# Low-rank mix in a fused attention and mixer kernel: second products placed two channel tiles at a time, sums of u issued later

## The chip, the cores and the metric

The kernel runs on one core of one Trainium2 chip. Its time is the device time of one execution in microseconds (us): 680.91 us, the median of three runs (680.91 to 682.74). The core has a matrix engine (PE, with its weight loads, PEld), a vector engine (DVE), a scalar engine (ACT), a general engine (POOL) and a queue that starts DMAs (SP). Each works through its own instructions in the order in which the program issues them, and they wait for each other through semaphores.

## The reference

Clustered attention over 2 batches of 768 tokens and 8 heads gives a tensor x of 2 x 768 x 512. Two mixers follow. The first ends with a channel mix, and the second has a low-rank token mix of rank 32 and a feed-forward with 2048 inner channels:

```
u = x + y                                  # first mixer, y from the token mix
x = u + relu(u @ w_ch)                     # channel mix
h = x^T @ U @ V                            # low-rank token mix: 768 -> 32 -> 768
u = x + h^T
out = u + relu(u @ w_ch1) @ w_ch2          # feed-forward
```

Everything is float32. A float32 product is made of three matmuls on reduced-precision halves (high with high, high with low, low with high).

## The kernel before, in words

x is kept as eight tiles xT[b * 4 + t], 128 channels by 768 tokens, four channel tiles t for each batch b. The change lies in the function mixer, in the stretch between the channel mix and the first products of the feed-forward. An order written out by hand decides there; no planner moves instructions. These helpers matter:

- chmix(b, e, mid), L582 and L587: 24 matmuls into two PSUM banks, one per half of the tokens, and then two DVE instructions that add the positive part to xT. In the middle of its matmuls it calls mid.
- turn(b, t), L600 and L601: six PE transposes of one channel tile into two banks, copied out by two ACT instructions.
- low1(b), L627 to L635: the first product of the low-rank mix, 48 small matmuls into one bank. ACT copies it out (L631, four instructions), DVE and ACT split it into halves (L633, L634, L635).
- low2(b, t), L644 and L646: the second product for one channel tile, two matmuls into a bank each, each added to xT by one DVE instruction.
- split_u(b, t), L651 and L652: ACT makes the high half of u (768 columns), POOL the low half.
- u_sum(0, i), L664: two DVE subtractions each, of tiles that both lie in SBUF. The sums 1 to 4 feed a seven-product scheme for 2 x 2 blocks (class Quartet, L744 and L752) whose first use is Quartet(1, 0). Sum 2 reads sum 1, and sum 4 reads sum 2.
- split_sum(0, i), L670 and L671: ACT makes the high half of a sum, POOL the low half.
- ff1(c, f, mid), L698 to L705: 12 matmuls into one bank (512 columns), then gh by ACT (L703) and gl by DVE (L705). The bank is free when gl is made.
- ff2(c, f), L717: three matmuls for each of four channel tiles e, into four banks that ff2(0, 0) takes and ff2(0, 1) gives back after its additions (L727).
- conv_step and conv_after: a background conversion of the next weights. conv_after holds finished steps that are still to be issued. Just ahead of chmix(1, 0) it holds three: three POOL additions (L467 to L469), and two splits, each an ACT instruction (L473) and a POOL instruction (L475).
- unit(n), L796: second products of a Quartet. unit(0) of Quartet(1, 0) reads g[0, 0] and g[1, 0], which POOL makes at L758.

PSUM has eight banks that are handed out in a ring: a new tile takes the bank that was handed out eight tiles earlier and waits until that one has been read. Only ff2 keeps its four banks out of the ring.

```
    ring = deque(range(8))
    def bank(name, keep=None):
        i = ring.popleft()
        if keep is None:
            ring.append(i)
```

Of the kernel before, what the change touches and what calls it, by code (L numbers as in the profile page):

```python
# [23 lines left out]
NP = 4  # L24
# [17 lines left out]
def tile_cluster_block(ctx: ExitStack, tc: tile.TileContext, qk, v, cent, wth, wr, wi, wch,  # L42
# [69 lines left out]
    def cols(hf):  # L112
        return slice(hf * HALF, (hf + 1) * HALF)
# [324 lines left out]
    def conv_until(dst, i):  # L438
        while i not in dst:
            assert conv_do or conv_in or conv_load or conv_after  # L440
            conv_step()
# [131 lines left out]
    def chmix(b, e, mid=None):  # L573
        ps = banks("h")
        n = 0
        for t in range(NP):
            if mid and t == 2:
                mid()
            wv = wcol(wch_t, t * DM + e * P, P)
            for a, c in PASSES:  # L580
                for hf in range(2):
                    nc.tensor.matmul(out=ps[hf][:, :HALF], lhsT=wv[a], rhs=xs[b, t][c][:, hf * HALF:(hf + 1) * HALF],  # L582
                                     start=(n == 0), stop=(n == 11))
                n += 1
        x = xT[b * NP + e]
        for hf in range(2):
            nc.vector.scalar_tensor_tensor(x[:, cols(hf)], ps[hf][:, :HALF], 0.0, x[:, cols(hf)], op0=ALU.max, op1=ALU.add)  # L587
# [4 lines left out]
    def turn(b, t):  # L592

        x = xT[b * NP + t]
        xt4[b, t] = slot(f"xt{t}", F32, [P, NT, P])
        for hf in range(2):
            ps = bank("tp")
            for j in range(3):
                st = 3 * hf + j
                nc.tensor.transpose(ps[:, j * P:(j + 1) * P], x[:, st * P:(st + 1) * P], ident)  # L600
            nc.scalar.activation(out=xt4[b, t][:, 3 * hf:3 * hf + 3].rearrange("p s d -> p (s d)"), in_=ps[:, :HALF],  # L601
                                 func=AF.Copy)
# [20 lines left out]
    def low1(b):  # L623
        ps = bank("h1")
        for st in range(NT):
            for t in range(NP):
                nc.tensor.matmul(out=ps[32 * t:32 * t + 32, :P], lhsT=uv["u"][:, st * RANK:(st + 1) * RANK],  # L627
                                 rhs=xt4[b, t][:, st], start=(st == 0), stop=(st == NT - 1))
        h1 = slot("h1")
        for t in range(NP):  # L630
            nc.scalar.activation(out=h1[0:32, t * P:(t + 1) * P], in_=ps[32 * t:32 * t + 32, :P], func=AF.Copy)  # L631
        hs = slot("h1s", F32R)
        nc.vector.tensor_copy(hs[0:32, :DM], h1[0:32, :DM])  # L633
        nc.vector.tensor_tensor(hs[64:96, :DM], h1[0:32, :DM], f32(hs[0:32, :DM]), op=ALU.subtract)  # L634
        nc.scalar.activation(out=hs[32:64, :DM], in_=h1[0:32, :DM], func=AF.Copy)  # L635
        h1s[b] = hs
# [50 lines left out]
    def ff1(c, f, mid=None):  # L687
        ps = bank("g")
        o = 0
        for b, s0, w in CHUNKS[c]:  # L690
            n = 0
            for t in range(NP):
                if mid and t == 2:
                    mid()
                conv_until(w1p_t, f)
                wv = [w[:, t * P:(t + 1) * P] for w in w1p_t[f]]
                for a, e in PASSES:
                    nc.tensor.matmul(out=ps[:, o:o + w], lhsT=wv[a], rhs=us[b, t][e][:, s0:s0 + w],  # L698
                                     start=(n == 0), stop=(n == 11))
                    n += 1  # L700
            o += w
        gh = tmp.tile([P, 512], F32R, tag="gh", name="gh")
        nc.scalar.activation(out=gh, in_=ps, func=AF.Relu)  # L703
        gl = tmp.tile([P, 512], F32R, tag="gl", name="gl")
        nc.vector.scalar_tensor_tensor(gl, ps, 0.0, f32(gh), op0=ALU.max, op1=ALU.subtract)  # L705
        gt[c, f] = (gh, gl)
# [309 lines left out]
    def mixer():  # L1016

        seq = [(u, st) for u in range(4) for st in range(NT)]
        LEAD = 2
        CONVERT = (*range(3, 16), 20, 21)  # L1020
        last = NG - 1
        for n in range(len(seq) + LEAD):
            if n < len(seq):
                theta(*seq[n])
                if 3 <= n < 22:
                    conv_step()
                theta_z(*seq[n])
            if n >= LEAD:
                ymix(*seq[n - LEAD])
            if n == 1:  # L1030
                row_sums(last)
            if n == 2:
                spread(last)
                norm_x(last)
            if n in CONVERT:
                conv_step()
            if n < len(seq):
                theta_lo(*seq[n])
            if n in CONVERT:
                conv_step()  # L1040
            if n in (9, 10):
                for t in range(2):
                    split_x(1, 2 * (n - 9) + t)
            if n == 11:
                conv_load.extend(weigh_in(wch, NP * DM, wch_t))
                c2 = weigh_in(w2, NF * DM, w2_t)
                ff = []
                for k in range(NQ):
                    if k < GF // 2:
                        ff.extend(Convert(w1, NF * DM, 2 * k + j, keep_split(w1p_t), width=DM) for j in range(2))  # L1050
                    else:
                        ff.extend(weigh_pair(k))
                    while c2 and c2[0].c0 < (k + 1) * 2 * DM:
                        ff.append(c2.pop(0))
                conv_load.extend(ff[:4])
                conv_load.append(Convert(u_in, NT * RANK, 0, [keep_u]))
                conv_load.append(Convert(v_in, S, 0, [keep_v, keep_vl], 32))
                conv_load.extend(ff[4:])
                conv_start()
            if 20 <= n <= 23:  # L1060
                split_x(0, n - 20)
            if n in (24, 25):
                split_x(1, n - 24, nc.gpsimd)

        for e in range(NP):
            chmix(0, e, lambda: e and turn(0, e - 1))
            if e in (0, 1):
                split_x(1, 2 + e)
            conv_step(3)
        conv_until(uv, "u")  # L1070
        conv_until(uv, "v")
        while conv_after:
            conv_after.popleft()()
        chmix(1, 0, lambda: turn(0, 3))
        low1(0)
        chmix(1, 1, lambda: turn(1, 0))
        conv_step(3)
        for t in range(NP):
            low2(0, t)
        for t in range(NP):  # L1080
            split_u(0, t)
        chmix(1, 2, lambda: turn(1, 1))
        u_sum(0, 1)
        u_sum(0, 2)
        chmix(1, 3, lambda: turn(1, 2))
        split_sum(0, 1, nc.gpsimd)
        split_sum(0, 2, nc.gpsimd)
        u_sum(0, 3)
        u_sum(0, 4)
        ff1(0, 0, lambda: turn(1, 3))  # L1090
        low1(1)
        split_sum(0, 3, nc.gpsimd)
        split_sum(0, 4, nc.gpsimd)
        ff1(0, 1)
        for t in range(NP):
            low2(1, t)
        ff2(0, 0)
        for t in range(NP):
            split_u(1, t)
        ff2(0, 1)  # L1100
        was = Quartet(1, 0)
        for n in range(7):
            was.step(n)
            if 0 < n < 6:
                conv_step()
        for j in range(2):
            ff1(1, j)
            was.unit(2 * j)
            was.unit(2 * j + 1)
            u_sum(1, j + 1)  # L1110
            conv_step()
        for j in range(2):
            ff1(2, j)
            u_sum(1, j + 3)
            ff2(1, j)
            split_sum(1, 2 * j + 1, nc.gpsimd)
            split_sum(1, 2 * j + 2, nc.gpsimd)
            conv_step()
        for n in (4, 5):
            was.unit(n)  # L1120
        conv_step()
        q = Quartet(1, 1)
        for n in range(7):
            q.step(n)
            if n in (1, 2):
                was.unit(5 + n)
            elif n in (4, 6):
                ff2(2, n // 2 - 2)
            if 0 < n < 6:
                conv_step()  # L1130
        was = q
        for k in range(2, NQ):
            for b in range(2):
                q = Quartet(k, b)
                for n in range(7):
                    q.step(n)
                    was.unit(n)
                    if 0 < n < 6:
                        conv_step()
                was.unit(7)  # L1140
                was = q
        for n in range(8):
            was.unit(n)
# [58 lines left out]
```

## Time and profile before

The profiled execution took 681.67 us, and its span from the first to the last instruction is 679.9 us. Busy time in the span:

| engine | busy us | share | instructions |
|---|---|---|---|
| PE | 665.9 | 98% | 4623 |
| PEld | 573.3 | 84% | 4624 |
| DVE | 466.2 | 69% | 820 |
| ACT | 357.0 | 53% | 726 |
| POOL | 290.1 | 43% | 290 |

The stretch of the change runs from about 396 us to 446 us. Matmuls are pipelined, so the duration of one overlaps the next; how far two starts lie apart says what a matmul costs. A bracket behind a row of the timeline gives the time for which the engine stood idle before it, and whose end it waited for.

### The profile page before, as it was taken

Reading aid. Unit: us, or ns where it says so; the run is one execution under the profiler, and the core shown is the slowest. Engines: PE = TensorE matmul, PEld = TensorE weight load, DVE = VectorE, ACT = ScalarE, POOL = GpSimd, SP = SyncE. Lnnn points to the kernel's source line nnn. Section 1 sums busy time; section 2 is a strip of 40 time slices with the busy share of each in tenths; the row PEclk is TensorE's granted clock in tenths of the full one; section 3 lists DMA queues with packets and bytes.
Section 4 is the critical chain, followed back from the end, with each engine's and each line's share of the span. In section 5 each row is a group of like instructions: output and inputs, shape, how many; then the busy total and the mean of one; then the engine's idle time right before and its main releaser. Section 6 shows DMA issues by size and latency. Waiting matters only on the chain.

```text
span 679.9 us, 12025 instructions
## 1 busy us (share of the span) xinstructions
PE 665.9 (98%) x4623; PEld 573.3 (84%) x4624; DVE 466.2 (69%) x820; ACT 357.0 (53%) x726; POOL 290.1 (43%) x290
## 2 busy tenths in 40 slices
PE   8899999999999999999999999999999999999998
PEld 3567766755765599999999998899999999999997
DVE  6888887897877367547475548768886666776554
ACT  8647656665776554456464444543454453543221
POOL 9423323233235324113223146757756664756221
PEclk9799999999999999999999999999999999999999
DMA  6769778576522102003101221021221222110013
GB/s 202 211 149 265 210 189 236 156 190 163 175 94 87 54 1 79 1 1 101 56 23 32 62 79 47 1 63 48 78 82 58 77 79 79 32 31 1 1 46 140
DMA packets 21785, 62.56 MB, mean 92 GB/s; under 512 B 4224, under 2 KB 7296, under 8 KB 21728
## 3 DMA queue, kind: packets, MB, share of 16 engines
q1 hardware_dynamic: 21728, 61.80, 31.8%
q8 instruction: 36, 0.59, 0.4%
q14 instruction: 21, 0.17, 0.1%
HBM read 40.35 MB, written 3.15 MB: 64 GB/s over the span
## 4 chain that ended last, share of the span: by engine, by line
PE 90%; ACT 4%; DVE 4%; issue 1%; DMA 1%; POOL 0%; SPq 0%; DVEq 0%; POOLq 0%
PE acc L796 17%; PE q L744 15%; PE y L562 15%; PE pv L316 9%; PE st L303 8%; PE l L335 5%; PE th L520 5%; PE h L582 4%; PE smax L251 3%; PE g L698 3%; PE acc L717 2%; DVE mx L255 2%; ACT p L308 2%; ACT hi L188 1%; PE th L524 1%
## 5 line engine op out<-in xcount | busy, mean ns | idle before, releaser
L796 PE MATMUL acc<-g,wh 128*128 128x384 f32 x448 | 113.8, 334 | 0.0
L255 DVE TENSOR_REDUCE mx<-smax 128x1 f32<-128x512 f32 x144 | 89.6, 682 | 21.9 <-PE smax L251 21.9
L308 ACT ACTIVATE p<-st 128x512 f32<-128x512 f32 x192 | 79.0, 513 | 44.5 <-PE st L303 43.9
L758 POOL TENSOR_TENSOR g<-sum,g 128x384 fp32r<-128x384 f32 x56 | 61.5, 1099 | 84.7 <-ACT g L757 84.7
L401 POOL TENSOR_TENSOR wl<-cv,wh 128x768 fp32r<-128x768 f32 (+1 forms) x31 | 55.3, 1785 | 95.8 <-ACT wh L397 51.0
L752 DVE TENSOR_TENSOR xT<-acc,xT 128x384 f32<-128x384 f32 x112 | 61.9, 555 | 46.4 <-PE acc L796 46.2
L562 PE MATMUL y<-wh,z 128*128 128x384 f32 x384 | 87.6, 340 | 0.3 <-ACT z L540 0.3
L796 PEld LDWEIGHTS acc<-g,wh 128*128 128x128 f32 x448 | 80.9, 188 | 0.1
L303 PE MATMUL st<-qp,kp 128*128 128x256 f32 (+1 forms) x384 | 79.8, 350 | 0.4 <-ACT qp L284 0.2
L796 PE MATMUL acc<-g,wl 128*128 128x384 f32 x224 | 74.8, 334 | 0.0
L303 PEld LDWEIGHTS st<-qp,kp 128*128 128x128 f32 x384 | 58.6, 193 | 19.0 <-issue 8.5
L756 ACT ACTIVATE sum<-sum 128x384 f32<-128x384 f32 x56 | 29.3, 524 | 82.8 <-DVE sum L752 82.8
L752 DVE TENSOR_TENSOR sum<-q,sum 128x384 f32<-128x384 f32 x98 | 53.1, 553 | 24.6 <-PE q L744 21.1
L562 PEld LDWEIGHTS y<-wh,z 128*128 128x128 f32 x384 | 67.0, 188 | 0.5 <-ACT z L540 0.5
L316 PE MATMUL pv<-p,v 128*32 128x384 f32 x768 | 66.2, 486 | 0.0
L546 POOL TENSOR_TENSOR z<-tht,z 128x256 fp32r<-128x256 f32 x24 | 19.3, 802 | 87.6 <-ACT z L540 87.5
L316 PEld LDWEIGHTS pv<-p,v 128*32 128x32 f32 x768 | 31.5, 110 | 29.6 <-issue 20.9
L392 DVE SCALAR_TENSOR_TENSOR cv<-cv,st 128x768 int32<-128x768 int32 (+3 forms) x47 | 49.3, 1049 | 3.2 <-ACT cv L385 2.6
L562 PE MATMUL y<-wl,z 128*128 128x384 f32 x192 | 48.8, 335 | 0.0
L251 PE MATMUL smax<-kp,qp 128*128 128x512 f32 x192 | 43.9, 347 | 3.0 <-ACT qp L177 1.9
L251 PEld LDWEIGHTS smax<-kp,qp 128*128 128x128 f32 x192 | 32.9, 191 | 12.9 <-issue 4.3
L796 PEld LDWEIGHTS acc<-g,wl 128*128 128x128 f32 x224 | 42.1, 188 | 0.0
(169 smaller groups left out, 1410.7 us busy)
## 6 DMA issues: line engine op xcount, KB each, us to landing
st<-in_w_dram SPq DMA_DIRECT2D x17, 512.0 KB, 3.5
st<-in_w_dram SPq DMA_DIRECT2D x10, 768.0 KB, 4.2
raw<-in_qk_dram SPq DMA_DIRECT2D x16, 384.0 KB, 5.0
qp<-hi SPq DMA_DIRECT2D x26, 192.0 KB, 3.0
st<-in_wr_dram SPq DMA_DIRECT2D x6, 768.0 KB, 4.6
st<-in_wi_dram SPq DMA_DIRECT2D x6, 768.0 KB, 4.3
kp<-hi SPq DMA_DIRECT2D x32, 96.0 KB, 3.0
qp<-lo SPq DMA_DIRECT2D x32, 96.0 KB, 2.7
```

The costliest lines, as they stand in the source:

```text
L251: nc.tensor.matmul(out=ps[:, c:c + w], lhsT=qp[s, h, 0][:, (a + j) * P:(a + j + 1) * P], rhs=kp[s, h, 0][:, k0:k0 + w], start=True, stop=True)
L255: nc.vector.tensor_reduce(mx_t[g, h][:, o:o + n], ps.rearrange("p (n w) -> p n w", n=n), axis=AX.X, op=ALU.max)
L303: nc.tensor.matmul(out=ps[:, c:c + n], lhsT=kp[s, h, w][:, (a + j) * P:(a + j + 1) * P], rhs=qp[s, h, w][:, q0:q0 + n], start=(w == 0), st ...
L308: nc.scalar.activation(out=pt[g, h, a + j][:, q0:q0 + n], in_=ps[:, c:c + n], func=AF.Exp, scale=float(D) ** -0.5)
L316: nc.tensor.matmul(out=pvt[g][hf][r:r + 32, :HALF], lhsT=v_t[g][:, kt, r:r + 32], rhs=pt[g, r // 64, kt][:, cols(hf)], start=(kt == 0), st ...
L392: nc.vector.scalar_tensor_tensor(t, t, 3, self.lw, op0=ALU.logical_shift_left, op1=ALU.bitwise_or)
L401: nc.gpsimd.tensor_tensor(t[:, :c.w], c.t, f32(c.hi[:, :c.w]), op=ALU.subtract)
L562: nc.tensor.matmul(out=yps[u, j][hf][:, :HALF], lhsT=lhs, rhs=w[st][e][:, hf * HALF:(hf + 1) * HALF], start=(st == 0 and n == 0), stop=(st ...
L744: nc.tensor.matmul(out=ps[:, :HALF], lhsT=w[a][:, j * P:(j + 1) * P], rhs=u_block(self.b, y, e, j), start=(n == 0), stop=(n == 5))
L752: nc.vector.tensor_tensor(out, ps[:, :HALF], x, op=ALU.add)
L758: nc.gpsimd.tensor_tensor(t[:, 1], r, f32(t[:, 0]), op=ALU.subtract)
L796: nc.tensor.matmul(out=ps[:, :HALF], lhsT=wv[a], rhs=self.g[i, hf][:, x], start=(m == 0), stop=(m == 5))
```

## The change

The waiting conversion steps (conv_after) are issued behind low1(0) instead of ahead of chmix(1, 0). The second products of batch 0 are issued two channel tiles at once and then singly, in the middle of chmix(1, 2) and behind it, each followed by its splits. All four sums of u move behind chmix(1, 3): sums 1 and 2 directly behind its additions, sums 3 and 4 behind low1(1), and the splits of the sums move along. The second products of batch 1 are divided in two pairs, one ahead of each ff2(0, j). No instruction is added or removed.

```
+        chmix(1, 0, lambda: turn(0, 3))
+        low1(0)
         while conv_after:
             conv_after.popleft()()
-        chmix(1, 0, lambda: turn(0, 3))
-        low1(0)
         chmix(1, 1, lambda: turn(1, 0))
         conv_step(3)
-        for t in range(NP):
+        for t in range(2):
             low2(0, t)
-        for t in range(NP):
+        for t in range(2):
             split_u(0, t)
-        chmix(1, 2, lambda: turn(1, 1))
+
+        def middle():
+            turn(1, 1)
+            low2(0, 2)
+
+        chmix(1, 2, middle)
+        low2(0, 3)
+        for t in range(2, NP):
+            split_u(0, t)
+        chmix(1, 3, lambda: turn(1, 2))
         u_sum(0, 1)
         u_sum(0, 2)
-        chmix(1, 3, lambda: turn(1, 2))
+        ff1(0, 0, lambda: turn(1, 3))
+        low1(1)
         split_sum(0, 1, nc.gpsimd)
         split_sum(0, 2, nc.gpsimd)
         u_sum(0, 3)
         u_sum(0, 4)
-        ff1(0, 0, lambda: turn(1, 3))
-        low1(1)
+        ff1(0, 1)
         split_sum(0, 3, nc.gpsimd)
         split_sum(0, 4, nc.gpsimd)
-        ff1(0, 1)
-        for t in range(NP):
-            low2(1, t)
-        ff2(0, 0)
-        for t in range(NP):
-            split_u(1, t)
-        ff2(0, 1)
+        for j in range(2):
+            for t in range(2 * j, 2 * j + 2):
+                low2(1, t)
+            ff2(0, j)
+            for t in range(2 * j, 2 * j + 2):
+                split_u(1, t)
```

## Rows read from the trace of the kernel before

**Rows 1.** The page's chain that ended last: share of the span by engine.

```profile
PE 90%; ACT 4%; DVE 4%; issue 1%; DMA 1%; POOL 0%; SPq 0%; DVEq 0%; POOLq 0%
```

**Rows 2.** Busy time by windows, behind the change: window and length, then each engine.

```profile
480.00:580.00 100.00, 100.00 (x577) 99.84 (x576) 69.72 (x120) 46.67 (x84) 60.00 (x53) 1.00 0.23 69
```

**Rows 3.** Timeline of PE, 396 to 446 us: start, duration, engine, line, count, idle before.

```profile
396.40 0.81 PE L600 MATMUL tp<-cst_sb,xT 128*128 128x128 f32 x6
...
399.24 0.42 PE L627 MATMUL h<-xt,cv 128*32 128x128 f32 x6
400.07 1.50 PE L627 MATMUL h<-xt,cv 128*32 128x128 f32 x42 [0.42 <-ACT xt L601]
401.50 0.61 PE L582 MATMUL h<-xh,wh 128*128 128x384 f32 x2
...
406.45 1.97 PE L644 MATMUL h<-vs,h1s 96*128 96x384 f32 x8
409.56 0.91 PE L582 MATMUL h<-xh,wh 128*128 128x384 f32 x2 [1.14 <-DVE xT L646]
410.30 0.51 PE L582 MATMUL h<-xl,wh 128*128 128x384 f32 x2
...
423.11 1.52 PE L627 MATMUL h<-xt,cv 128*32 128x128 f32 x48
424.56 0.50 PE L698 MATMUL g<-uh,wh 128*128 128x512 f32 x1
...
427.46 1.38 PE L644 MATMUL h<-vs,h1s 96*128 96x384 f32 x7
429.53 0.45 PE L644 MATMUL h<-vs,h1s 96*128 96x384 f32 x1 [0.69 <-DVE gl L705]
430.00 0.50 PE L717 MATMUL acc<-gh,wh 128*128 128x512 f32 x1
...
435.60 0.34 PE L744 MATMUL q<-uh,wh 128*128 128x384 f32 x1
...
445.75 0.51 PE L796 MATMUL acc<-g,wh 128*128 128x384 f32 x2
```

**Rows 4.** Timeline of PE's weight loads behind chmix(1, 1), which ends at 406.45.

```profile
407.16 0.19 PEld L644 LDWEIGHTS h<-vs,h1s 96*128 96x128 f32 x1 [0.17 <-DVE xT L587]
407.62 0.47 PEld L644 LDWEIGHTS h<-vs,h1s 96*128 96x128 f32 x3 [0.28 <-DVE xT L587]
```

**Rows 5.** Timeline of ACT around low1(0).

```profile
398.80 0.84 ACT L473 ACTIVATE wh<-cv 128x768 fp32r<-128x768 f32 x1 [0.55 <-POOL cv L469]
399.55 0.85 ACT L601 ACTIVATE xt<-tp 128x384 f32<-128x384 f32 x2
```

**Rows 6.** Timeline of DVE, 408 to 429 us.

```profile
408.95 3.80 DVE L646 TENSOR_TENSOR xT<-h,xT 128x384 f32<-128x384 f32 x8
...
418.83 1.02 DVE L664 TENSOR_TENSOR t<-xT,t 128x384 f32<-128x384 f32 x2
...
426.34 0.68 DVE L634 TENSOR_TENSOR h1s<-h,h1s 32x512 fp32r<-32x512 f32 x1
428.79 0.69 DVE L705 SCALAR_TENSOR_TENSOR gl<-g,gh 128x512 fp32r<-128x512 f32 x1 [1.76 <-ACT gh L703]
```

**Rows 7.** Single L664 and L652 instructions that overlap: ns min/median/max, first and last start.

```profile
L664 DVE TENSOR_TENSOR t<-xT x1: 2189/2189/2189, 416.7 to 416.7; 128x384 f32<-128x384 f32 x1
L652 POOL TENSOR_TENSOR ul<-xT,uh x1: 2152/2152/2152, 416.3 to 416.3; 128x768 fp32r<-128x768 f32 x1
```

**Rows 8.** Timeline of POOL, 427 to 432 us.

```profile
427.48 3.63 POOL L671 TENSOR_TENSOR u0t<-t,u0t 128x768 fp32r<-128x768 f32 x2 [3.65 <-ACT u0t L670]
```

**Rows 9.** The page's costliest groups, two of POOL: busy, mean ns, idle before.

```profile
L758 POOL TENSOR_TENSOR g<-sum,g 128x384 fp32r<-128x384 f32 x56 | 61.5, 1099 | 84.7 <-ACT g L757 84.7
L401 POOL TENSOR_TENSOR wl<-cv,wh 128x768 fp32r<-128x768 f32 (+1 forms) x31 | 55.3, 1785 | 95.8 <-ACT wh L397 51.0
```

**Rows 10.** Windows around two changes of the granted TensorE clock (third value from the end).

```profile
19.20:19.40 0.20, 0.00 (x0) 0.00 (x0) 0.13 (x1) 0.04 (x1) 0.19 (x1) 0.70 1.03 277
26.00:26.20 0.20, 0.20 (x3) 0.20 (x2) 0.20 (x1) 0.12 (x1) 0.00 (x0) 0.74 1.02 231
```

## The prediction

> **What bounds the kernel now.** I read the page's chain first: 90% of it is PE [rows 1], so only what lets PE start its next matmul earlier can count. Then the windows behind the change: from 480 to 580 us PE is busy for 100.00 of 100.00 us [rows 2]. A gain made ahead of that is kept to the end, unless it is lost again at a new wait. Third, the timeline of PE through the stretch of the change [rows 3]. There the reader is to see three places where PE stood still:
>
> - low1(0) takes from 399.24 to 401.50, 2.26 us, waiting for ACT's copy L601 of turn(0, 3); low1(1), which waits for nothing, takes from 423.11 to 424.56, 1.45 us. Lost: 0.81 us.
> - From low2(0) at 406.45 to the second pair of matmuls of chmix(1, 2) at 410.30 lie 3.85 us. Eight low2 matmuls at 0.173 us (seven in 1.38 us, the last of them lasting some 0.35) and one pair, 0.35, would be 1.73 us. Lost: 2.1 us, since eight low2 tiles take the whole ring, and the next bank is free only after DVE's first addition L646.
> - low2(1) and ff2(0, 0) begin at 427.46 and 430.00, 2.54 us apart, for 1.39 us of matmuls. Lost: 1.15 us, by the wait for gl (L705), whose bank the eighth matmul takes.
>
> So there are about 4.1 us to be had, 0.6% of 680.91. The sum below is made against the profiled execution (681.67 us, span 679.9, so 1.77 us around it) and carried over to the median, 0.76 us lower. A measurement of this kernel can tell 0.3%, 2.04 us, from no change.
>
> **The change, part by part.** (1) conv_after behind low1(0). Before, L473 of the conversion (from 398.80, 0.84 us) stands ahead of L601 in ACT's order, and L601 starts only at 399.55 [rows 5]. The transposes are over by 397.21 [rows 3], so without L473 in front low1(0) finds its input: gain 0.81 us, bounds 0.4 to 0.81. The two L473 now run after low1(0)'s L635, ahead of the copy of turn(1, 0), which nobody needs before low1(1); their POOL halves then end some 4 us ahead of the next POOL work.
>
> (2) low2(0) in pieces. With four low2 matmuls ahead of it, chmix(1, 2) takes the banks of chmix(1, 1), which DVE reads at L587. Those banks were free 0.71 and 1.17 us after the last matmul of chmix(1, 1): the weight loads at 407.16 and 407.62 against 406.45 [rows 4]. Four low2 matmuls cover 0.69 us. The first matmul of chmix(1, 2) waits for nothing, the second about 0.3 us, and the first after a wait costs some 0.1 more: 0.4 us lost instead of 2.1, gain 1.7. low2(0, 2) in the middle needs banks that L646 read over 2.2 us earlier; no wait. But chmix(1, 3) is now in the place where chmix(1, 2) was: it takes the banks of chmix(1, 2), whose L587 come 0.71 and 1.17 us after its end, and only the two matmuls of low2(0, 3), 0.35 us, lie between. That is a new loss of 0.75 us (bounds 0.4 to 1.0). Together with (1) ff1(0, 0) starts 0.81 + 1.7 - 0.75 = 1.75 us earlier.
>
> (3) Sums 1 and 2 behind chmix(1, 3). DVE is free, and POOL's four L652 are over by then, so they run in some 1 us a pair [rows 6]. They end before gl of ff1(0, 0) can be made: cost nothing. If POOL were still at work each of the four would wait for it, up to 1.6 us each, and only the later ones would reach gl.
>
> (4) Sums 3 and 4 behind low1(1): this is where the gain goes. Count from the end of low1(1) (424.56 before). Here a DVE subtraction of two SBUF tiles and a POOL subtraction do not run together: the one at 416.7 took 2.19 us while POOL worked, against two in 1.02 us while POOL stood still [rows 6, 7], and the next POOL instruction took 2.15 us instead of 1.82 [rows 7, 8]. They take turns, one whole instruction each. Before, sums 3 and 4 met POOL's L671 while PE had other work. Now L670 of sums 1 and 2 follow L635, so POOL begins L671 at +2.92 (as L671 of sum 3 did: 427.48 - 424.56 [rows 3, 8]). DVE is done with L634 at +2.46 (426.34 + 0.68 [rows 6]) and has four subtractions behind it. The first runs from +2.4 to +2.95, the second is ready at +2.87, ahead of POOL by 0.05, and I give it the turn: it ends at +3.4. POOL's first L671 then holds to +5.2, the third subtraction ends at +5.7, POOL's second at +7.5, the fourth at +7.95. Only then comes gl of ff1(0, 1) (0.69): +8.6. Bounds for the four: 2.0 us if they never meet POOL, and four turns, ending at +9.8, if POOL gets the first; I take +7.95, between them, since rows 7 show one turn per instruction and the start of POOL is the only doubt.
>
> The Trainium skill, "SBUF — State Buffer", section "Who interferes with whom", says that DVE's second read port is GpSimd's too and that whoever issues first keeps it for its whole instruction. By that rule the second subtraction, issued first, wins as I have it; no row here shows a start this close.
>
> Who waits for that gl? low2(1) now takes four banks and ff2(0, 0) the next four, and its fourth (e = 3) is the one that ff1(0, 1) filled, the same bank for which the eighth low2 matmul waited before [rows 3]. PE from the end of low1(1): ff1(0, 1) to +2.90 (427.46 - 424.56), four low2 0.7, nine matmuls of ff2 at 0.23 us (24 from 430.00 to 435.60) 2.1: at +5.7 it stands before e = 3 and waits until +8.65, 2.95 us. Three matmuls after a wait, 0.8: +9.45. The second pair of low2(1) needs the banks of the first, and their four L646 start only behind gl at 0.475 us each (eight in 3.80 [rows 6]): the last bank is free at +10.5, low2 is through at +10.8, and ff2(0, 1), 12 x 0.23, ends at +13.6. Before it ended at 435.60, +11.05. That stretch is 2.55 us longer.
>
> (5) Sum: -1.75 + 2.55 = +0.8 us; worked with unrounded starts it is +0.65, and I take +0.7. What follows: POOL starts its eight subtractions (four L671, four L652, 1.82 us each) at +3.4, with two turns of DVE between, and is through at +18.9. About 1 us of conversion work on DVE may come in between; L758, L401 and L758 follow, 1.10 + 1.79 + 1.10 by their means [rows 9]. g[1, 0] is ready near +23.9. unit(0) began at 445.75, +21.2, and needs it 0.5 us later [rows 3], now at +24.25. It just holds; up to 0.3 us more is possible. Forecast: 680.91 + 0.7 = **681.6 us**, no difference that can be measured.
>
> **Rivals.** *A: POOL gets the first turn* (the slower side). If L671 is ahead of the second subtraction, three of DVE's four have to wait for a POOL instruction instead of two, and the fourth ends at +9.8, because by then L671 of sum 3 is ready as well. PE's wait grows by 1.85 us: +2.5, 683.4 us. For it: the two starts lie 0.05 us apart. Against it: DVE's comes first. It decides from the moment at which POOL's start precedes +2.87.
>
> *B: the clock falls in the wait.* The granted clock fell to half (1.2 GHz) at 19.3 us, after some 6 us in which PE was fed at the pace of DVE's maxima, and was back at 2.4 GHz at 26.1 us [rows 10]. The wait of 1.14 us at 409.56 [rows 3] did not lower it. A wait of 2.95 us lies between these. If it falls, the matmuls that follow run at half pace: over 6.8 us at half, as there, 3.4 us are lost, over half of that 1.7, in part beside the wait for L646. Time: 683.0 to 685.0, and up to 686.8 together with A. The Trainium skill ("TensorE: Matmul & The Clock Gate", "Part 1") says that the throttled state is the default and activity lifts it, which by itself points to B.
>
> *C: no meeting at the port.* If DVE's four subtractions run through in 2 us, gl is ready at +5.1 and PE never waits: -1.75 - 1.15 = -2.9 us at Quartet(1, 0). But POOL has become late: its L671 used to start ahead of low1(1) and now starts after it, so eight subtractions from +2.92 or, behind DVE's four, from +4.35, and 4.0 us more, give g[1, 0] at +21.5 to +22.9, where unit(0) would want it at +20.55 (21.7 less 1.15). PE waits 0.95 to 2.35 us there: 679.0 to 680.4 us. Against it: rows 7.
>
> *D: less than claimed in (1) and (2)*, the copies or L587 still late: up to 0.8 us of the gain gone, 682.4 us.
>
> **How the numbers follow.** Forecast 0.45; A alone 0.1; B, with or without A, 0.23; C 0.14; D 0.08. Faster by over 0.3% (below 678.87) would take C at its very best and a larger gain in (2): 0.06. Slower by over 0.3% (above 682.95): A, nearly all of B, and a few parts in a hundred from D and the forecast: 0.36. The rest, 0.58, is no difference. The range reaches down to C, 679.2, and up through B, 685.0.
>
> **What would show it.** In the trace after: low1(0) in 1.45 us; a wait of PE's L582 for L587 at chmix(1, 3); two or three of the four L664 of sums 3 and 4 at about 2 us; one wait of some 3 us of L717 for gl L705; L646 one by one ahead of the second low2 pair; POOL without a gap from the first L671 to L758. If L717 doesn't wait for L705 by over 2 us, step (4) is wrong; a granted clock under 1.00 near 430 us shows B; a wait of L796 for L758 shows C.

## The result: slower by 0.7%

The changed kernel takes 686.54 us (median of six runs, 683.35 to 687.52) against 681.47 us for the kernel before: ratio 1.0066, 95% interval 1.0042 to 1.009. Run again beside the experiments it took 685.38 us against 682.2, ratio 1.0046 (1.0029 to 1.0063). The profiled execution took 687.52 us with a span of 685.5 us.

Executions differ by one or two us ahead of the change already, so the traces are compared by stretches between fixed starts on PE: from turn(0, 3) to ff1(0, 0), from there to Quartet(1, 0), and on to ff1(1, 1), which follows unit(0) and unit(1). "Difference" is the sum of the three against the kernel before. The last column sets the times of each kernel against those of the kernel before that ran beside it.

| kernel | to ff1(0, 0) | to Quartet(1, 0) | to ff1(1, 1) | difference | ratio of times (95%) |
|---|---|---|---|---|---|
| before | 23.21 | 15.99 | 12.24 | | |
| the change | 21.46 | 21.99 | 12.25 | +4.26 | 1.0066 (1.0042 to 1.009) |
| e0, the change again | 21.46 | 22.12 | 12.24 | +4.38 | 1.0046 (1.0029 to 1.0063) |
| e1, sums first | 21.46 | 14.86 | 13.71 | -1.41 | 0.9985 (0.9965 to 1.0006) |
| e2, wait filled | 21.94 | 19.89 | 12.25 | +2.64 | 1.003 (1.0019 to 1.0042) |
| e3, front alone | 21.50 | 19.94 | 12.26 | +2.26 | 1.0017 (1.0004 to 1.003) |
| e4, back alone | 23.19 | 19.86 | 12.25 | +3.86 | 1.0044 (1.003 to 1.0058) |
| e5, first split early | 21.46 | 15.03 | 12.26 | -2.69 | 0.9955 (0.9943 to 0.9968) |
| e6, pair behind | 21.00 | 15.03 | 12.25 | -3.16 | 0.9946 (0.9934 to 0.9958) |
| e7, splits late | 21.46 | 15.00 | 16.32 | +1.34 | 1.0014 (1.0 to 1.0027) |
| e8, sum 3 first | 21.46 | 15.74 | 13.14 | -1.10 | 0.9974 (0.9965 to 0.9984) |

The front of the change gains 1.75 us, the stretch behind it loses 6.00. Behind ff1(1, 1) nothing differs: from 480 to 580 us PE is busy for 100.00 of 100.00 us, as in [rows 2].

The profile after, timeline of PE, answers to [rows 3]: start, duration, line, count, idle before.

```profile
400.57 1.52 PE L627 MATMUL h<-xt,cv 128*32 128x128 f32 x48
...
413.35 0.51 PE L644 MATMUL h<-vs,h1s 96*128 96x384 f32 x2
413.98 0.91 PE L582 MATMUL h<-xh,wh 128*128 128x384 f32 x2
...
422.71 1.52 PE L627 MATMUL h<-xt,cv 128*32 128x128 f32 x48
424.16 0.50 PE L698 MATMUL g<-uh,wh 128*128 128x512 f32 x1
...
429.59 0.40 PE L717 MATMUL acc<-gh,wl 128*128 128x512 f32 x1
434.20 0.80 PE L717 MATMUL acc<-gh,wh 128*128 128x512 f32 x1 [4.21 <-DVE gl L705]
...
435.65 1.48 PE L644 MATMUL h<-vs,h1s 96*128 96x384 f32 x4
436.93 0.63 PE L717 MATMUL acc<-gh,wh 128*128 128x512 f32 x1
```

low1(0) is now one block of 1.5 us. One wait is left that matters, 4.21 us ahead of the fourth tile (e = 3) of ff2(0, 0), and what follows it is slow: a matmul of L717 lasts 0.63 us instead of 0.40. The same stretch on DVE, which answers to [rows 6]:

```profile
425.97 0.68 DVE L634 TENSOR_TENSOR h1s<-h,h1s 32x512 fp32r<-32x512 f32 x1
426.68 2.69 DVE L664 TENSOR_TENSOR t<-xT,xT 128x384 f32<-128x384 f32 x2
429.30 4.25 DVE L664 TENSOR_TENSOR t<-xT,t 128x384 f32<-128x384 f32 x2
433.47 0.68 DVE L705 SCALAR_TENSOR_TENSOR gl<-g,gh 128x512 fp32r<-128x512 f32 x1
434.07 1.93 DVE L646 TENSOR_TENSOR xT<-h,xT 128x384 f32<-128x384 f32 x4
```

and the single subtractions of POOL, then those of DVE, from narrow windows of the timeline:

```profile
427.09 1.86 POOL L671 TENSOR_TENSOR u0t<-t,u0t 128x768 fp32r<-128x768 f32 x1 [7.99 <-ACT u0t L670]
428.91 2.15 POOL L671 TENSOR_TENSOR u0t<-t,u0t 128x768 fp32r<-128x768 f32 x1
431.01 2.12 POOL L671 TENSOR_TENSOR u0t<-t,u0t 128x768 fp32r<-128x768 f32 x1
```

```profile
427.16 2.22 DVE L664 TENSOR_TENSOR t<-xT,xT 128x384 f32<-128x384 f32 x1
429.30 2.17 DVE L664 TENSOR_TENSOR t<-xT,t 128x384 f32<-128x384 f32 x1
```

They alternate, one instruction each, and POOL's first started 0.07 us ahead of DVE's second (427.09 and 427.16). The windows around the fall and the rise of the clock, which answer to [rows 10] (third value from the end):

```profile
432.60:433.00 0.40, 0.00 (x0) 0.00 (x0) 0.40 (x1) 0.00 (x0) 0.40 (x1) 1.00 0.00 0
433.00:433.50 0.50, 0.00 (x0) 0.00 (x0) 0.50 (x2) 0.00 (x0) 0.13 (x1) 0.82 0.00 0
...
434.00:436.00 2.00, 1.80 (x5) 1.51 (x6) 2.00 (x5) 1.27 (x2) 1.50 (x1) 0.50 0.00 0
...
440.00:440.20 0.20, 0.20 (x2) 0.20 (x1) 0.20 (x1) 0.00 (x0) 0.20 (x1) 0.64 0.00 0
```

The granted clock falls to half (1.2 GHz) at about 433.3 us, inside the wait, and is back at 2.4 GHz at about 440.1 us.

### The profile page after: what moved, and what is told of

It reads as the page before. It is cut to its first block, busy times and chain, and to the rows that moved or that the text cites. A ratio compares the mean times of both kernels' runs of the same rounds, so it can differ in the third digit from the quotient of the medians.

```text
span 685.5 us, 12027 instructions
## 1 busy us (share of the span) xinstructions
PE 669.9 (98%) x4624; PEld 575.6 (84%) x4624; DVE 467.3 (68%) x820; ACT 356.5 (52%) x726; POOL 290.0 (42%) x290
## 4 chain that ended last, share of the span: by engine, by line
PE 89%; DVE 4%; ACT 4%; POOL 1%; issue 0%; DMA 0%; SPq 0%; POOLq 0%
PE acc L796 17%; PE q L744 15%; PE y L562 15%; PE pv L316 9%; PE st L303 8%; PE h L582 5%; PE l L335 5%; PE th L520 5%; PE smax L251 3%; PE acc L717 2%; PE g L698 2%; DVE mx L255 2%; ACT p L308 2%; DVE t L664 1%; ACT hi L188 1%; PE tp L600 1%
## 5 line engine op out<-in xcount | busy, mean ns | idle before, releaser
L796 PE MATMUL acc<-g,wh 128*128 128x384 f32 x448 | 113.8, 334 | 0.0
L758 POOL TENSOR_TENSOR g<-sum,g 128x384 fp32r<-128x384 f32 x56 | 61.4, 1098 | 85.4 <-ACT g L757 85.4
L401 POOL TENSOR_TENSOR wl<-cv,wh 128x768 fp32r<-128x768 f32 (+1 forms) x31 | 55.4, 1785 | 95.8 <-ACT wh L397 50.9
L796 PEld LDWEIGHTS acc<-g,wh 128*128 128x128 f32 x448 | 80.9, 188 | 0.1
L796 PE MATMUL acc<-g,wl 128*128 128x384 f32 x224 | 74.8, 334 | 0.0
L796 PEld LDWEIGHTS acc<-g,wl 128*128 128x128 f32 x224 | 42.1, 188 | 0.0
```

The lines of the kernel that those rows point to most:

```text
L401: nc.gpsimd.tensor_tensor(t[:, :c.w], c.t, f32(c.hi[:, :c.w]), op=ALU.subtract)
L758: nc.gpsimd.tensor_tensor(t[:, 1], r, f32(t[:, 0]), op=ALU.subtract)
L796: nc.tensor.matmul(out=ps[:, :HALF], lhsT=wv[a], rhs=self.g[i, hf][:, x], start=(m == 0), stop=(m == 5))
```

## Experiments

Theory M: DVE's subtractions of sums 3 and 4 and POOL's L671 do not run together but take turns, gl of ff1(0, 1) is late, PE waits for its bank, and in that wait the clock falls. "A subtraction meets POOL" stands below for one such turn. Rival R: the division of low2(1) around ff2(0, 0) takes the ring's banks too early, whatever the sums do.

**e0: the change once more.**

> The changed kernel once more, beside the others. Theory M (turns at the port, then the clock): DVE's second subtraction of sum 3 comes after POOL's start, three of the four subtractions take some 2.2 us, L717 waits about 4.2 us for gl, and the granted clock falls to half for some 7 us. Time near 686.5 us, or near 683.4 in an execution whose clock doesn't fall. Rival R (the ring alone: ff2(0, 0) takes the bank of g(0, 1) too early, whatever the sums do) expects the same of this run.

685.38 us; the same wait of 4.2 us and a fall of the clock, as both theories had it.

**e1: sums 3 and 4 directly behind sums 1 and 2.**

```
         u_sum(0, 2)
+        u_sum(0, 3)
+        u_sum(0, 4)
         ff1(0, 0, lambda: turn(1, 3))
...
-        u_sum(0, 3)
-        u_sum(0, 4)
         ff1(0, 1)
```

> Only sums 3 and 4 move, directly behind sums 1 and 2. POOL stands still then. M: all eight subtractions in about 3.8 us, gl of ff1(0, 1) ready some 4.9 us after low1(1), L717 doesn't wait, the clock stays at 1.00. Then POOL is late (its first L671 still comes 2.9 us after low1(1)) and L796 waits 1 to 2 us for L758 at unit(0). Time 679.5 to 680.5 us. R: L717 still waits over 2 us for L705, time above 683 us.

680.47 us against 682.2, and 685.38 for the change beside it; by the interval not yet apart from before (one of its eleven executions took 687.91 us, and no trace of that one was taken), by the stretches 1.41 us less. L717 waits for nothing, and the clock stays at 1.00: R falls, since the banks are taken in the same order. Timeline of DVE and then of PE in e1:

```profile
419.00 1.02 DVE L664 TENSOR_TENSOR t<-xT 128x384 f32<-128x384 f32 x2
...
421.81 1.02 DVE L664 TENSOR_TENSOR t<-xT,t 128x384 f32<-128x384 f32 x2
```

```profile
443.07 0.52 PE L796 MATMUL acc<-g,wh 128*128 128x384 f32 x2
444.15 0.44 PE L796 MATMUL acc<-g,wl 128*128 128x384 f32 x1 [0.56 <-POOL wl L401]
444.43 0.34 PE L796 MATMUL acc<-g,wh 128*128 128x384 f32 x1
445.12 0.44 PE L796 MATMUL acc<-g,wh 128*128 128x384 f32 x1 [0.35 <-POOL g L758]
```

The subtractions start 0.47 us apart, and the next wait shows: unit(0) waits for POOL's L401 and L758, 0.9 us of idle time and 1.47 us on the stretch (13.71 for 12.24).

**e8: only sum 3 moved, sum 4's two subtractions stay.**

```
         u_sum(0, 2)
+        u_sum(0, 3)
         ff1(0, 0, lambda: turn(1, 3))
...
-        u_sum(0, 3)
         u_sum(0, 4)
```

> The changed kernel with sum 3 directly behind sums 1 and 2; only sum 4's two subtractions are left where POOL starts L671. M: one of them meets POOL and ends 5.2 us after low1(1) instead of 9.4, gl at 5.9; L717 waits 0 to 0.3 us, the second low2 pair some 0.6 us for L646, the clock stays at 1.00; L796 waits about 1 us. Half a microsecond above e1, about 1.2 us below the kernel before. If the wait doesn't go by the number of turns, L717 waits over 2 us.

680.48 us against 681.92. The two subtractions took 2.69 us together, so one of them met POOL; the loads of L717 waited 0.5 us for gl and those of the second low2 pair 0.7 us for L646. Up to Quartet(1, 0) that is 0.88 us more than with all four moved (15.74 for 14.86 in e1). Timeline of DVE in e8:

```profile
425.28 2.69 DVE L664 TENSOR_TENSOR t<-xT,t 128x384 f32<-128x384 f32 x2
```

**e7: the sums in place, the splits of sums 1 and 2 later.**

```
         low1(1)
-        split_sum(0, 1, nc.gpsimd)
-        split_sum(0, 2, nc.gpsimd)
         u_sum(0, 3)
         u_sum(0, 4)
         ff1(0, 1)
+        split_sum(0, 1, nc.gpsimd)
+        split_sum(0, 2, nc.gpsimd)
```

> The changed kernel with its sums where they are, but the splits of sums 1 and 2 behind ff1(0, 1): this takes POOL away from beside DVE, not DVE from beside POOL. M: sums 3 and 4 take 2 us, gl of ff1(0, 1) ends 5.1 us after low1(1), L717 doesn't wait. POOL starts L671 1.7 us later than in the changed kernel, so L796 at unit(0) waits 2 to 3 us for L758, twice as long as in e1; 0 to 1 us below the kernel before, and about 2 more if the clock falls in that wait. If something other than the meeting of L664 and L671 holds gl up, L717 still waits about 4 us.

683.56 us against 681.92. With POOL out of the way the four subtractions take 2 us where they stood, and L717 waits for nothing: it is the meeting, not the place of the sums. But POOL starts at 428.40, and L796 waits at two places, 1.63 us in all (less than the 2 to 3 expected), after which the clock falls. Timelines of DVE and of PE in e7:

```profile
426.42 1.03 DVE L664 TENSOR_TENSOR t<-xT,xT 128x384 f32<-128x384 f32 x2
427.36 1.02 DVE L664 TENSOR_TENSOR t<-xT,t 128x384 f32<-128x384 f32 x2
```

```profile
444.80 0.44 PE L796 MATMUL acc<-g,wh 128*128 128x384 f32 x1 [0.29 <-POOL g L758]
446.58 0.51 PE L796 MATMUL acc<-g,wl 128*128 128x384 f32 x1 [1.34 <-POOL wl L401]
446.88 1.35 PE L796 MATMUL acc<-g,wh 128*128 128x384 f32 x2
```

**e2: the wait of the change filled with matmuls of zeros.**

```
+            if (c, f, e) == (0, 0, 3):
+                for _ in range(18):
+                    nc.tensor.matmul(out=aps[c, 2], lhsT=fill_t["z"][:, :P], rhs=fill_t["z"][:, :512],
+                                     start=False, stop=False)
...
+        fill_t["z"] = slot("zero", BF16)
+        nc.gpsimd.memset(fill_t["z"][:, :512], 0.0)
```

> The changed kernel with 18 matmuls of zeros by zeros (128x512 bf16, some 0.22 us each) added into the open sum of e = 2 ahead of e = 3, so that PE works for 3.9 of the 4.2 us of its wait. M (the wait lets the clock fall, and that costs time of its own): DVE and POOL as in the changed kernel, gl at the same place, the clock at 1.00 behind it; from the first matmul of e = 3 to Quartet(1, 0) 4.2 us instead of 7.0. Time some 2.7 us below a run of the changed kernel with the fall, 682.5 to 684 us. If the matmuls behind the wait would wait for L646 anyway, the time stays near 685.4 us.

684.25 us against 681.9. (Lines behind the edit are a few higher: L722 is L717 of the change.) Timeline of PE in e2, and a window behind the wait (the clock is the third value from the end):

```profile
429.08 4.06 PE L719 MATMUL acc<-zero 128*128 128x512 bf16 x18
433.42 0.51 PE L722 MATMUL acc<-gh,wh 128*128 128x512 f32 x1 [0.27 <-DVE gl L706]
...
434.23 1.49 PE L644 MATMUL h<-vs,h1s 96*128 96x384 f32 x4
435.55 0.39 PE L722 MATMUL acc<-gh,wh 128*128 128x512 f32 x1
```

```profile
434.00:435.00 1.00, 0.97 (x5) 0.56 (x3) 1.00 (x3) 0.68 (x1) 1.00 (x1) 1.00 0.00 0
```

gl comes no earlier (again some 10 us behind low1(1)), the clock stays at 1.00, and from e = 3 to Quartet(1, 0) it takes 4.93 us (433.42 to 438.35) instead of 6.99. So the fall costs 2.1 us in this pair of traces, not the 2.7 expected; the times alone do not tell e2 from the change (their intervals overlap). The reason for the smaller price: the second low2 pair waits for its L646 at either clock, 1.3 us for four matmuls. Some 0.5 us were lost ahead of that (21.94 for 21.46): beside the zeros' memset on POOL, DVE's L388 took 1.46 us instead of 0.99 in the change.

**e3: the front alone** (conv_after and low2(0) as in the change, all else in the order of before; the cut shows two of the places against the change).

```
         chmix(1, 2, middle)
         low2(0, 3)
         for t in range(2, NP):
             split_u(0, t)
+        u_sum(0, 1)
+        u_sum(0, 2)
         chmix(1, 3, lambda: turn(1, 2))
+        split_sum(0, 1, nc.gpsimd)
...
```

> The first half of the change alone: conversion steps behind low1(0), low2(0) in pieces; sums, splits and low2(1) in the order of before. M: from turn(0, 3) to ff1(0, 0) PE takes 1.7 us less than before, then loses some 0.5 us at turn(1, 3), since sums 1 and 2 meet L652 and hold up L587; behind it as before. Time 1.0 to 1.8 us below the kernel before, 679.7 to 680.5 us. If the pieces themselves were the loss, it would be above the kernel before.

A miss: 683.43 us against 682.2, 0.2% slower. The gain up to ff1(0, 0) is there (21.50), but three of the four subtractions of sums 1 and 2 meet a POOL instruction, and I had priced the delay at 0.5 us. Timeline of DVE, and of PE, in e3:

```profile
413.07 2.78 DVE L664 TENSOR_TENSOR t<-xT 128x384 f32<-128x384 f32 x2
415.78 4.29 DVE L664 TENSOR_TENSOR t<-xT,t 128x384 f32<-128x384 f32 x2
419.99 1.01 DVE L587 SCALAR_TENSOR_TENSOR xT<-h,xT 128x384 f32<-128x384 f32 x2
```

```profile
420.59 1.50 PE L600 MATMUL tp<-cst_sb,xT 128*128 128x128 f32 x6 [1.98 <-DVE xT L587]
421.74 0.77 PE L698 MATMUL g<-uh,wh 128*128 128x512 f32 x1
422.31 0.63 PE L698 MATMUL g<-ul,wh 128*128 128x512 f32 x1
```

The channel mix's last addition L587 comes 2.9 us after the chmix(1, 3) that feeds it (ff1(0, 0) starts at 417.06), turn(1, 3) waits 1.98 us, and the clock falls there too (0.63 us a matmul). So the front's gain needs sums 1 and 2 behind the last addition, as the change has them.

**e4: the back alone** (the order of before up to chmix(1, 3), the order of the change from there).

> The second half of the change alone: the order of before up to chmix(1, 3), the order of the change behind it. M: the same meeting of sums 3 and 4 with L671, L717 waits about 4.2 us for gl, the clock falls; 5 to 6 us more than before, 686.5 to 688 us. If the loss came from the conversion steps or from low2(0) in pieces, it would be near the kernel before.

685.56 us against 681.9, a little below the expectation: the loss belongs to the back, but L717 waited 2.58 us, not 4.2. Timelines of PE, POOL and DVE in e4:

```profile
432.57 0.51 PE L717 MATMUL acc<-gh,wh 128*128 128x512 f32 x1 [2.58 <-DVE gl L705]
```

```profile
427.16 8.25 POOL L671 TENSOR_TENSOR u0t<-t,u0t 128x768 fp32r<-128x768 f32 x4 [9.37 <-ACT u0t L670]
```

```profile
427.16 0.55 DVE L664 TENSOR_TENSOR t<-xT,xT 128x384 f32<-128x384 f32 x1
427.63 4.29 DVE L664 TENSOR_TENSOR t<-xT,t 128x384 f32<-128x384 f32 x2
```

Here POOL and DVE's second subtraction start at the same 427.16, and DVE gets the turn: two meetings, not three, and gl ends 8.36 us behind low1(1) instead of 9.99. The clock fell all the same: to half from some 434.5 to 437.9 us, behind that wait and short ones of the second low2 pair (0.7 us in all).

**e5 and e6: towards a version that beats both.** e5 takes e1 and starts POOL earlier; e6 is e5 with low2(0, 2) beside low2(0, 3). The first part of the cut is that of e5 against e1, the second what e6 adds (it stands earlier in the program).

```
         ff1(0, 0, lambda: turn(1, 3))
-        low1(1)
         split_sum(0, 1, nc.gpsimd)
+        low1(1)
         split_sum(0, 2, nc.gpsimd)
...
-        chmix(1, 2, middle)
+        chmix(1, 2, lambda: turn(1, 1))
+        low2(0, 2)
         low2(0, 3)
```

> As e1 (all four sums directly behind chmix(1, 3)), and the split of sum 1 ahead of low1(1), so that POOL starts L671 some 2.7 us earlier. M: no wait of L717, no wait of L796; the waits that are left are those of chmix(1, 2) and chmix(1, 3) for L587. 2.9 us below the kernel before (1.0 us below e1). If the wait of L796 in e1 doesn't hang on when POOL starts, the time is that of e1.

> As e5, and low2(0, 2) stands behind chmix(1, 2), beside low2(0, 3), so that four matmuls instead of two lie between chmix(1, 2) and chmix(1, 3). M: the wait of chmix(1, 3) for L587 shrinks from 0.75 to 0.4 us, as at chmix(1, 2); 0.35 us below e5, some 3.2 us below the kernel before. If L646 of low2(0, 2) now delays L587, it is no faster than e5.

e5: 679.37 us, e6: 678.69 us, against 681.9, ratios 0.9955 and 0.9946. Neither L717 nor L796 waits in either. From turn(0, 3) to ff1(0, 0) e6 needs 0.46 us less than e5; their times lie too close together to be told apart. e6 is the fastest kernel here, 0.5% ahead of the kernel before. Timeline of POOL in e6, where L671 starts as low1(1) ends (421.82), not 2.9 us behind it:

```profile
421.89 1.85 POOL L671 TENSOR_TENSOR u0t<-t,u0t 128x768 fp32r<-128x768 f32 x1 [4.30 <-ACT u0t L670]
...
441.15 1.02 POOL L758 TENSOR_TENSOR g<-sum,g 128x384 fp32r<-128x384 f32 x1
```

## Why the prediction was wrong, point by point

The forecast of 681.6 us and its upper end of 685.0 were too low. Its first three steps held, the fourth found the right mechanism and priced it too low, and two rivals, A and B, came together.

- **(1) and (2)**: forecast -1.75 us up to ff1(0, 0), measured 21.46 - 23.21 = -1.75. low1(0) no longer waits. The new wait at chmix(1, 3) is there: its two loads wait 0.45 and 0.28 us for L587 (a loss of 0.75 was forecast).
- **(3)**: sums 1 and 2 took 2 us in all and delayed nothing. e3 shows what they would have cost in the old place.
- **(4)** is the step that failed. I had written: "the second is ready at +2.87, ahead of POOL by 0.05, and I give it the turn". I let the first subtraction overlap the end of L634, and it did not. It started at +2.52 (426.68 - 424.16), L634 ending at +2.49, the second at +3.00, and POOL's L671 at +2.93, as forecast to 0.01 us. Three meetings followed instead of two, and the fourth subtraction ended at +9.39 instead of +7.95. That is rival A, to which I gave 0.1; e4 shows the other outcome of the same race, 2.58 us of wait for 2.95 forecast. I should have given a race within 0.1 us about even chances. The Trainium skill ("SBUF — State Buffer", "Who interferes with whom") gives the port that DVE's second input shares with POOL to whoever issues first; by POOL's lead of 0.07 us the trace agrees (0.06 in e2: 426.32 and 426.38), and at equal starts (e4) DVE had it. The runs show the turns, not the port itself.
- **Rival B** came with it, and this is a second failure of the sum, which put the clock at nothing. I gave B 0.23 because a wait of 1.14 us had not lowered the clock; but in e4, where the race went as forecast, the wait of 2.58 us was followed by a fall too, and the back took 3.87 us more than before (19.86 for 15.99) instead of 2.55; the sum was too low even without A. e2 prices the fall of the change at 2.1 us, near the lower of my two values (1.7 and 3.4).
- The sum of the back, worked again: 2.55 as forecast, 1.44 for the lost turn (9.39 - 7.95) and 2.1 for the clock make 6.1; measured 6.00. With -1.75 in front it is +4.25. (e2, with the clock kept up, has the first two terms alone: 19.89 - 15.99 = 3.90, against 3.99.) The forecast had +0.7 and named 686.8 for A with B; the range stopped at 685.0.
- **(5) and rival C**: POOL did become the next bound as soon as DVE's sums no longer met it (e1, e7), and starting it earlier removes that (e5). In the change itself POOL is hidden by the loss.

In six executions of the change the one with the highest mean clock (0.997; the others 0.990 to 0.993) took 683.35 us, which is rival A without the fall, 683.4. No trace of that execution was taken, and the mean clock of the kernel before varies too (0.995 to 0.997), so this is no proof.

## What to carry to other kernels

A DVE instruction with two SBUF inputs that stands ahead of a bank's release should not be issued where POOL begins a run of long instructions: each can cost a whole POOL instruction (here 2.2 us for one that takes 0.55 alone), and the bank ring hands the delay to PE. When such sums are moved, ask what POOL starts at that moment, and then whether POOL itself still finishes in time. Where two engines start within 0.1 us of each other, price both orders; and give a wait of PE as long as those behind which the clock fell here (1.98 to 4.21 us) the price of the clock as well as its own.

## What the runs showed that was not expected

The clock fell after a single wait of 1.98 us (e3), after 2.58 us with short waits behind it (e4) and after waits of 0.29 and 1.34 us with one matmul between (e7), while 1.14 us did not lower it in the kernel before. It stayed at half for 3 to 4 us in e3, e4 and e7, and for some 7 us in the change. Matmuls of zeros kept it up (e2). And a POOL memset, which reads nothing, seems to have held up DVE's L388 for about half a microsecond in e2: L388 took 1.46 us, and 0.99 in the change, where no memset stands; in both it ended 0.42 us behind POOL's last instruction beside it (L475 in the change, the memset in e2).
